# Half of a layer's weights loaded and narrowed later, more places for experts' weights, and an integer in the cosine's range reduction

## The chip, the core and the metric

One core of a Trainium2 chip. A kernel's time is the device time of one execution in microseconds, and what counts is the median of the runs. A profiled execution leaves a trace: its span runs from the first to the last instruction. Engines: PE multiplies matrices (PEld is its weight load), DVE and ACT work on vectors, SP issues the DMAs here.

## The reference

Three stages follow one another. q, k, v are 4 x 12 x 448 x 64, w1 8 x 768 x 1024, w2 8 x 1024 x 768, w_in 768 x 2048 and w_out 2048 x 768; w_in and w_out come as float64.

```python
scores = q @ k.T / sqrt(64) - log(448)
x = sigmoid(scores) @ v                     # 4 x 12 heads, then tokens: 1792 x 768
logits = x @ phi                            # 1792 x 32 slots, 8 experts of 4 slots
d = softmax(logits, axis=0); slots = d.T @ x
slot_out[e] = relu(slots[e] @ w1[e]) @ w2[e]   # 8 experts
x = softmax(logits, axis=1) @ slot_out      # combine weights c
h = x @ w_in
out = (h * cos(h)) @ w_out
```

The kernel never forms the second x: it multiplies slot_out (32 x 768) with w_in to m (32 x 2048), and gets h of 128 features and 448 tokens with one matmul of m and the turned combine weights.

## The kernel before

**Attention, about 0 to 157 us.** 24 pairs of heads, each with scores (L397), a sigmoid on ACT (L405) and the product with v (L416). A planner (`Plan`) gets operations with a cost and their predecessors, simulates the engines and emits each engine's instructions in the order of its simulation; `RANK` says which kind goes first. Into this order `fill(t)`, called twice for each pair, puts half loads of weights (`load_half`, 512 KB) and narrowing steps of w_in. A float64 is narrowed to float32 by one ACT instruction (L266) and three of DVE (L269, L270, L273) on pieces of 512 columns: 24 pieces for the whole of w_in. The places for loads are a pool of `W_SLOTS` tiles of 1 MB, through which raw w_in and then w1 pass; a place is free again when its w_in is narrowed. Narrowed w_in stays in `wi`, 48 KB of each partition.

**Experts, about 157 to 243 us.** The list `wloads` gives the order of all loads, `spots` the place of each. Seven more loads follow when attention leaves its memory (three places a, one more w, ct, m4 and zone); from there on each load waits for a place that PE has read. `w1_group` (L974) and `w2_rows` (L1010) run over two groups of four experts. `turn_weights` (L299, L305, L308) turns the combine weights of a batch; it stands inside group 1's loop over w1.

**Last layer, from about 245 us.** `wide_m` (L938) multiplies the features 0 to 511 of m, `rest_m` (L947) the other 1536, in four column blocks of 384; the latter are split into a high and a low part and spread over m4's partitions by 16 DMAs (`spread`, L1152). A unit is 128 features of one batch of 448 tokens. Its wave: `hidden` (L1208, PE), `scaled` (L1181, ACT: turns plus a quarter), `rounded` (L1184, ACT: adds 1.5 x 2^23), `centred` (L1188, DVE), `sined` (L1193, ACT), `times` (L1198 or L1200, DVE); from unit 4 on g is split into two fp16 halves, `upper` (L1217, ACT) and `lower` (L1221, DVE). Then `out_tile` (L1243) adds six tiles of w_out times g in six PSUM banks, one fp32 product for the units 0 to 3 and three fp16 products afterwards. A second planner orders all this; waves are put in three units ahead of their tiles, and hidden values take turns in two PSUM banks.

Rows of w_out are loaded into six places, narrowed (`wo_abs`, `wo_steps`) and split into fp16 (`wo_hi` L1122, `wo_lo` L1125), each once, ahead of the first unit that uses it. The order of units decides when: features 0 to 3 of batch 0, 0 to 5 of batch 1, all 16 of batch 2, the rest of batch 0, the rest of batch 1, all of batch 3. Where the batch changes, six banks are evicted (L1266 adds an earlier sum, L1270 to L1274 don't), and finished ones go out. `bound` to `keep_powers` work out a power of two that g is scaled with.

Of the kernel before, what the change touches and what calls it, by code (L numbers as in the profile page):

```python
# [12 lines left out]
U32 = mybir.dt.uint32  # L13
AF = mybir.ActivationFunctionType
# [20 lines left out]
W_SLOTS, A_SLOTS = 15, 3  # L35
# [7 lines left out]
W_SCALE, G_BITS = 8.0, 14  # L43
F64_SCALE = 2.0 ** -112
# [18 lines left out]
class Op:  # L63
# [11 lines left out]
class Plan:  # L75
# [3 lines left out]
    RINGS = {"sc": 3}  # L79
# [81 lines left out]
def fused(ctx: ExitStack, tc: tile.TileContext, qk, vv, phi, w1, w2, w_in, w_out, out):  # L161
# [8 lines left out]
    bias_s = const.tile([P, 1], F32, name="bias_s")  # L170
    run_z = const.tile([P, 1], F32, name="run_z")
# [12 lines left out]
    wloads = [("wi", 0, c, k) for c in range(KD) for k in range(2)]  # L184
# [5 lines left out]
    spots = ["w"] * (2 * KD + W_SLOTS - LATE) + slots_a[0:1] + ["w"] * LATE + slots_a[1:] + ["ct", "m4", "zone"]  # L190
# [3 lines left out]
    wloads.insert(2 * KD + W_SLOTS + A_SLOTS + 2, wloads.pop(2 * KD + 2 * KD - 1))  # L194
# [116 lines left out]
    with ExitStack() as at:  # L311
# [371 lines left out]
        pieces = [(c, n) for c in range(KD) for n in range(DFF // CV)]  # L683
# [9 lines left out]
        def attention():  # L693
# [184 lines left out]
        with tc.manual_schedule():  # L878
# [8 lines left out]
            nc.gpsimd.memset(bias_s, neg_log_s)  # L887
            warm = const.tile([P, 1], F32, name="warm")
# [64 lines left out]
    def slots_of(c):  # L953

        if c < 4:
            return l_all[:, 256 + c * NS:256 + (c + 1) * NS]
        return s_acc[:, 512 + (c - 4) * NS:512 + (c - 3) * NS]

    with ExitStack() as ex:
# [3 lines left out]
        with tc.manual_schedule():  # L963
# [133 lines left out]
    more_wo.append(ctx.enter_context(reuse("more_wo", bufs=1, side="right")))  # L1097
    stg = ctx.enter_context(reuse("stg", bufs=3))
# [46 lines left out]
    mh, ml = [ring[:, (12 + k) * S:(12 + k) * S + 3 * P] for k in range(2)]  # L1145

    def spread(js, groups):

        for j in js:
            cols = slice(MC + 3 * P * j, MC + 3 * P * (j + 1))  # L1150
            for g in groups:
                nc.sync.dma_start(  # L1152
                    out=m4[g * NS:(g + 1) * NS, cols].bitcast(F32), in_=(mh, ml)[g // 2][j * NS:(j + 1) * NS]
                )

    def m_split_hi():
        nc.scalar.copy(mh.bitcast(F32R), m_ps[2][:, 0:3 * P])
        spread([0], (0, 1))

    def m_split_lo():  # L1160
        nc.vector.tensor_sub(ml.bitcast(F32R), m_ps[2][:, 0:3 * P], mh)
        spread([0], (2, 3))
        spread(range(1, 4), range(4))

    SOME, PLAIN = (4, 6), 4
    units = [(t, f) for t in range(2) for f in range(SOME[t])] + [(2, f) for f in range(NF)]
    units += [(t, f) for t in range(2) for f in range(SOME[t], NF)]
    units += [(t, f) for t in range(3, B) for f in range(NF)]
# [4 lines left out]
    def buf(k):  # L1173
        return ring[:, k * S:(k + 1) * S]
# [329 lines left out]
```

## Time and profile before

| | us |
|---|---|
| median of 3 runs (493.5 to 493.74) | 493.56 |
| the profiled execution | 494.58 |
| its span | 492.7 |
| PE busy | 467.9 |
| DVE busy | 330.4 |
| ACT busy | 291.4 |

[...] The share of busy time is a mean over three stages with different limits, and a matmul's end is modelled: what a change is worth is read in its stage.

### The profile page before, as it was taken

The page shows a single profiled execution, that of the slowest core. Times are in us where ns is not written, and L with a number is a line of the kernel's source. Part 1 is how long each engine was busy: PE and PEld are TensorE (multiplying, and loading weights), DVE is VectorE, ACT ScalarE, POOL GpSimd, SP SyncE. Part 2 cuts the span into 40 slices and gives each one's busy share as a digit, 9 for nine tenths or more (in the row PEclk, how much of TensorE's full clock was granted, in tenths as well). Part 3 has the DMA queues.
Part 4 walks back from the last instruction along what each step waited for, and adds up shares of the span by engine and source line. Part 5 has one row for each costly group of instructions (what it writes and reads, how often), then busy time and mean ns, then how long its engine had stood idle before and what let it go on. Part 6 is the DMA issues. An engine that isn't in the chain of part 4 may idle for free.

```text
span 492.7 us, 11063 instructions
## 1 busy us (share of the span) xinstructions
PE 467.9 (95%) x4564; PEld 248.7 (50%) x4564; DVE 330.4 (67%) x665; ACT 291.4 (59%) x508; POOL 0.7 (0%) x7
## 2 busy tenths in 40 slices
PE   7999989999999998687899999999999999999996
PEld 5665556566566332223455555555555555555553
DVE  4898879999986155000189999999845575575553
ACT  5887848968864012000269889886756556655562
POOL 0000000000000000000000000000000000000000
PEclk9999999999999998989999999999999999999999
DMA  8989979989848999999944631300300030030003
GB/s 279 365 305 338 310 258 323 351 250 363 274 175 296 395 414 414 414 416 405 396 159 122 243 120 73 129 1 2 112 1 0 1 112 2 1 113 0 1 0 113
DMA packets 33442, 99.12 MB, mean 201 GB/s; under 512 B 3568, under 2 KB 17520, under 8 KB 33392
## 3 DMA queue, kind: packets, MB, share of 16 engines
q1 hardware_dynamic: 33392, 98.42, 54.7%
q8 instruction: 36, 0.59, 0.5%
q14 instruction: 14, 0.11, 0.1%
HBM read 92.11 MB, written 5.51 MB: 198 GB/s over the span
## 4 chain that ended last, share of the span: by engine, by line
PE 71%; DMA 17%; DVE 8%; ACT 2%; issue 1%; SPq 0%; ACTq 0%
PE o L1243 45%; DMA w<-in_w 13%; PE av L416 9%; PE sc L397 5%; PE h L1208 3%; DMA v<-in_vv 2%; PE h L974 2%; PE sl L635 2%; DMA raw<-in_qk 2%; DVE lo L378 1%; ACT a L405 1%; PE o L1228 1%; DVE xt L426 1%; PE m L947 1%; DVE hi L375 1%
## 5 line engine op out<-in xcount | busy, mean ns | idle before, releaser
L1243 PE MATMUL o<-gh,wh 128*128 128x448 f16 x360 | 127.4, 354 | 0.0
L1243 PE MATMUL o<-gl,wh 128*128 128x448 f16 x360 | 126.9, 352 | 0.0
L1243 PE MATMUL o<-gh,wl 128*128 128x448 f16 x360 | 126.9, 352 | 0.0
L1243 PEld LDWEIGHTS <-wh 128*128 128x128 f16 x720 | 70.3, 98 | 71.8 <-issue 11.1
L405 ACT ACTIVATE a<-sc,bias_s 128x896 f32<-128x896 f32 x72 | 71.2, 1008 | 26.7 <-PE sc L397 19.4
L416 PE MATMUL av<-a,v 128*64 128x224 f32 x576 | 60.4, 357 | 2.6 <-DMA v<-in_vv 1.7
L1221 DVE TENSOR_TENSOR gl<-wi,gh 128x448 f16<-128x448 f32 x60 | 37.4, 623 | 32.7 <-ACT gh L1217 32.2
L1217 ACT CAST gh<-wi 128x448 f16<-128x448 f32 x60 | 33.7, 562 | 41.9 <-PE o L1243 31.1
L416 PEld LDWEIGHTS av<-a,v 128*64 128x64 f32 x576 | 39.3, 137 | 22.9 <-issue 4.1
L1200 DVE SCALAR_TENSOR_TENSOR wi<-h,scales,wi 128x448 f32<-128x448 f32 x60 | 40.9, 681 | 13.6 <-ACT wi L1193 12.3
L1243 PEld LDWEIGHTS <-wl 128*128 128x128 f16 x360 | 35.3, 98 | 28.1 <-issue 0.6
L1193 ACT ACTIVATE wi<-wi 128x448 f32<-128x448 f32 x63 | 36.2, 575 | 21.8 <-DVE wi L1188 21.6
L1188 DVE SCALAR_TENSOR_TENSOR wi<-wi 128x448 f32<-128x448 f32 x63 | 39.2, 622 | 12.9 <-ACT wi L1184 12.9
L1010 PE MATMUL so<-w,zone 128*32 128x256 f32 (+1 forms) x256 | 36.2, 534 | 9.6 <-DMA w<-in_w 9.5
L1184 ACT ACTIVATE wi<-wi 128x448 f32<-128x448 f32 x63 | 36.3, 577 | 1.7
L1181 ACT ACTIVATE wi<-h 128x448 f32<-128x448 f32 x63 | 33.7, 535 | 5.0 <-PE h L1208 4.9
L397 PE MATMUL sc<-hi 64*64 64x448 f16 (+1 forms) x384 | 33.6, 337 | 2.9 <-ACT a L405 2.1
L397 PEld LDWEIGHTS <-hi 64*64 64x64 f16 x768 | 24.9, 106 | 21.9 <-issue 13.3
L1208 PE MATMUL h<-ct,m 128*128 128x448 f32 x64 | 33.6, 525 | 0.3 <-DVE m L1143 0.3
L397 PE MATMUL sc<-lo,hi 64*64 64x448 f16 (+1 forms) x384 | 33.0, 326 | 0.1
L397 PE MATMUL sc<-hi,lo 64*64 64x448 f16 (+1 forms) x384 | 32.9, 326 | 0.0
L1041 DVE COPY l_all<-ps_so 128x64 f32<-128x64 f32 x2 | 0.4, 224 | 47.9 <-PE ps_so L1034 47.9
(174 smaller groups left out, 543.8 us busy)
## 6 DMA issues: line engine op xcount, KB each, us to landing
w<-in_w SPq DMA_DIRECT2D x28, 768.0 KB, 15.4
w<-in_w SPq DMA_DIRECT2D x30, 512.0 KB, 5.7
wi<-in_w_in SPq DMA_DIRECT2D x24, 512.0 KB, 7.3
wo<-in_w_out SPq DMA_DIRECT2D x16, 768.0 KB, 5.9
w<-in_w SPq DMA_DIRECT2D x11, 1024.0 KB, 9.3
raw<-in_qk SPq DMA_DIRECT2D x48, 224.0 KB, 5.2
v<-in_vv SPq DMA_DIRECT2D x24, 224.0 KB, 4.8
out_t<-wi SPq DMA_DIRECT2D x24, 224.0 KB, 2.0
```

The lines of the kernel that those rows point to most:

```text
L397: nc.tensor.matmul(ps[to, j, 0:cols.stop - cols.start], keys[at, first:first + D], q[at, cols], **flags)
L405: nc.scalar.activation(a, ps, AF.Sigmoid, bias=bias_s, scale=qk_scale)
L416: nc.tensor.matmul(av[i][rows[j], k, 0:S // 2], v32[i][at, vc:vc + D], a[at, j, sides[k] if g < 3 else slice(0, S // 2)], start=g == 0, st ...
L1010: nc.tensor.matmul(e2[g, k][j * NS:(j + 1) * NS, 0:n], h1[g][:, c, j * NS:(j + 1) * NS], w(j), start=c == 0, stop=c == F // P - 1,)
L1181: nc.scalar.activation(tmp[u][0][:, cols], hs[u][:, cols], AF.Copy, bias=0.25, scale=inv2pi)
L1184: nc.scalar.activation(tmp[u][1][:, cols], tmp[u][0][:, cols], AF.Copy, bias=magic)
L1188: nc.vector.scalar_tensor_tensor(out=ph[:, cols], in0=tn[:, cols], scalar=-magic, in1=ph[:, cols], op0=ALU.add, op1=ALU.subtract)
L1193: nc.scalar.activation(tmp[u][1][:, cols], tmp[u][0][:, cols], AF.Sin, scale=-2.0 * math.pi)
L1200: nc.vector.scalar_tensor_tensor(out=g[:, cols], in0=hs[u][:, cols], scalar=g_scale, in1=tn[:, cols], op0=ALU.mult, op1=ALU.mult)
L1208: nc.tensor.matmul(h, m4[:, f * P:(f + 1) * P], ct4[:, t * S:(t + 1) * S], start=True, stop=True)
L1221: nc.vector.tensor_sub(gs[u][2], gs[u][0], gs[u][1])
L1243: nc.tensor.matmul(ps, w[:, cols], g, start=begins(u) and n == 0, stop=ends(u) and n == len(terms) - 1)
```

## The change

- w_in's first half (features 0 to 1023, `EARLY` = 8 blocks) goes through attention as before; `wi` shrinks to 24 KB of each partition, and `W_SLOTS` grows from 15 to 18. Six loads less stand ahead of w1 in `wloads`. `fill` narrows 12 pieces instead of 24 at half the pace, and its half loads have the pace 1 instead of 9/8 for each t.
- w_in's second half is loaded in the last layer, six chunks of 1 MB through two places: two right at its start, the others when a place has been narrowed. Twelve pieces are narrowed there, after the units 20 and 25 of the emission order. `late_products` multiplies them, three chunks at a time, `late_add` sums, `late_hi` and `late_lo` split and spread over m4.
- `rest_m` has four blocks of 128 columns.
- Units: features 0 to 3 of batch 0, 0 to 7 of batch 1, 4 to 7 of batch 0, 0 to 7 of the batches 2 and 3, then 8 to 15 of the batches 3, 2, 1, 0. That makes nine stretches instead of six; each batch's last stretch adds to the earlier sum on DVE, and all other evictions are ACT's.
- The scale is worked out twice, for each half of the features.
- The cosine: `turns` writes h / 2 pi + 1/4 as int32 (ACT), `centred` takes h / 2 pi minus that integer (DVE, from PSUM), the sine adds pi / 2 from a pointer operand. `rounded` goes, and a wave has two buffers instead of three.
- `turn_weights` moves from group 1 of w1 to the first two calls of `w2_rows`.

```diff
-W_SLOTS, A_SLOTS = 15, 3
+W_SLOTS, A_SLOTS = 18, 3
+EARLY = NF // 2
+LATE_W, LATE_C = (NF - EARLY) * P // 4, 3
+SCALE_AT, LATE_AT = 1, {20: range(3), 25: range(3, 6)}
...
-    wi = wip.tile([P, KD, DFF], F32, name="wi")
+    wi = wip.tile([P, KD, EARLY * P], F32, name="wi")
...
-    wloads = [("wi", 0, c, k) for c in range(KD) for k in range(2)]
+    wloads = [("wi", 0, c, 0) for c in range(KD)]
...
-                while len(done) < min(len(pieces), 23 * t // 44):
+                while len(done) < min(len(pieces), 23 * t // 88):
                     narrows(len(done))
-                while len(half) < min(2 * len(pieces) + 4, 4 + 9 * t // 8):
+                while len(half) < 4 + t:
                     h = len(half)
                     k = h // 2 - W_SLOTS
-                    if h >= 2 * (W_SLOTS - LATE + 2 * KD) or 2 * k + 1 >= len(done):
+                    if h >= 2 * (W_SLOTS - LATE + KD) or 2 * k + 1 >= len(done):
                         return
...
         for j in range(4):
-            at = MC + 3 * P * j
+            at = MC + P * j
             nc.tensor.matmul(
-                m_ps[2][j * NS:(j + 1) * NS, 0:3 * P], so, wi[:, c, at:at + 3 * P],
+                m_ps[2][j * NS:(j + 1) * NS, 0:P], so, wi[:, c, at:at + P],
...
+    def late_products(c):
+        ps = late_ps[c] = ps_h.tile([P, 512], F32, tag="h", name=f"late_m{c}")[:, 0:LATE_W]
+        for k in range(c + 1 - LATE_C, c + 1):
+            for j in range(4):
+                nc.tensor.matmul(
+                    ps[j * NS:(j + 1) * NS], both[k], late_w[k][:, j * LATE_W:(j + 1) * LATE_W],
+                    start=k == c + 1 - LATE_C, stop=k == c,
+                )
...
-    def scaled(u, cols):
-        nc.scalar.activation(tmp[u][0][:, cols], hs[u][:, cols], AF.Copy, bias=0.25, scale=inv2pi)
-    def rounded(u, cols):
-        nc.scalar.activation(tmp[u][1][:, cols], tmp[u][0][:, cols], AF.Copy, bias=magic)
+    def turns(u, cols):
+        nc.scalar.activation(tmp[u][1][:, cols].bitcast(I32), hs[u][:, cols], AF.Copy, bias=0.25, scale=inv2pi)
 
     def centred(u, cols):
...
         nc.vector.scalar_tensor_tensor(
-            out=ph[:, cols], in0=tn[:, cols], scalar=-magic, in1=ph[:, cols], op0=ALU.add, op1=ALU.subtract
+            out=ph[:, cols], in0=hs[u][:, cols], scalar=inv2pi, in1=tn[:, cols].bitcast(I32),
+            op0=ALU.mult, op1=ALU.subtract,
         )
 
     def sined(u, cols):
-        nc.scalar.activation(tmp[u][1][:, cols], tmp[u][0][:, cols], AF.Sin, scale=-2.0 * math.pi)
+        nc.scalar.activation(tmp[u][1][:, cols], tmp[u][0][:, cols], AF.Sin, bias=quarter, scale=2.0 * math.pi)
...
+        def late(c):
+            x = Op("sp", 2.5, lambda: late_load(c), [wide.get((c - 2, 1))]) if c > 1 else None
+            for n in range(2):
+                x = Op("act", .58, lambda n=n: late_narrow(c, n), [x, wide.get(c // LATE_C - 1)])
+                for cost in (.35, .605, .605):
+                    x = Op("dve", cost, lambda: late_steps[c].pop(0)(), [x])
+                wide[c, n] = x
...
             tiles(u, range(2))
+            if u == SCALE_AT:
+                scaling(0)
+            for c in LATE_AT.get(u, ()):
+                late(c)
             if u + 3 < n_units:
                 wave_ops(u + 3)
...
         for f in range(A_SLOTS, WO_SLOTS):
             load_wo(f)
+        for c in range(2):
+            late_load(c)
```

## Rows read from the trace of the kernel before

**Rows 1.** Page, the 40 slices: busy tenths of PE, and GB/s.

```profile
PE   7999989999999998687899999999999999999996
...
GB/s 279 365 305 338 310 258 323 351 250 363 274 175 296 395 414 414 414 416 405 396 159 122 243 120 73 129 1 2 112 1 0 1 112 2 1 113 0 1 0 113
```

**Rows 2.** Page, chain that ended last, by engine.

```profile
PE 71%; DMA 17%; DVE 8%; ACT 2%; issue 1%; SPq 0%; ACTq 0%
```

**Rows 3.** Windows: from:to us, length, busy (xcount) by engine, PEclk, DMA share, GB/s.

```profile
20.00:140.00 120.00, 114.84 (x2125) 71.61 (x2123) 109.32 (x283) 93.50 (x152) 0.00 (x0) 1.00 0.89 307
152.00:190.00 38.00, 37.06 (x396) 15.23 (x392) 17.89 (x39) 4.85 (x11) 0.00 (x0) 1.00 1.02 406
190.00:239.00 49.00, 37.95 (x263) 12.99 (x262) 3.14 (x7) 1.61 (x4) 0.00 (x0) 0.93 1.02 408
246.00:347.80 101.80, 101.80 (x541) 53.86 (x542) 96.67 (x158) 85.47 (x154) 0.00 (x0) 1.00 0.30 104
347.80:400.00 52.20, 52.20 (x274) 26.83 (x272) 32.13 (x53) 31.37 (x61) 0.00 (x0) 1.00 0.15 54
```

**Rows 4.** Page, DMA issues of weights.

```profile
w<-in_w SPq DMA_DIRECT2D x30, 512.0 KB, 5.7
wi<-in_w_in SPq DMA_DIRECT2D x24, 512.0 KB, 7.3
```

**Rows 5.** Groups by shape, DVE, 0 to 163 us: busy us, mean ns, idle before.

```profile
L270 DVE SCALAR_TENSOR_TENSOR wi<-wi,wi 128x512 uint32<-128x512 uint32 x24 | 16.4, 682 | 0.3
L273 DVE SCALAR_TENSOR_TENSOR wi<-wi,wi 128x512 uint32<-128x512 uint32 x24 | 16.3, 680 | 0.2
...
L269 DVE TENSOR_SCALAR wi<-wi 128x512 uint32<-128x512 uint32 x24 | 10.0, 418 | 3.0 <-ACT wi L266 3.0
```

**Rows 6.** Timeline of PE, two waits: start us, us, what, [idle before].

```profile
20.73 2.49 PE L416 MATMUL av<-a,v 128*64 128x224 f32 x24 [0.63 <-DMA v<-in_vv]
...
44.01 2.49 PE L416 MATMUL av<-a,v 128*64 128x224 f32 x24 [1.04 <-DMA v<-in_vv]
```

**Rows 7.** Timeline, start of the last layer.

```profile
252.34 1.47 PE L947 MATMUL m<-wi,s_acc 128*32 128x384 f32 x16
...
254.86 0.62 DVE L1198 TENSOR_TENSOR wi<-h,wi 128x448 f32<-128x448 f32 x1
...
256.32 0.92 PE L1243 MATMUL o<-wi,wo 128*128 128x448 f32 x2
...
257.17 0.38 PE L1294 MATMUL scale<-ident,scales 128*1 128x128 f32 x2
```

**Rows 8.** Timelines of PE and DVE, units 4 to 25 of the last layer.

```profile
271.77 0.35 PE L1243 MATMUL o<-gh,wh 128*128 128x448 f16 x1
...
299.27 0.95 DVE L1125 SCALAR_TENSOR_TENSOR wl<-wo,wh 128x768 f16<-128x768 f32 x1
...
345.94 0.62 DVE L1221 TENSOR_TENSOR gl<-wi,gh 128x448 f16<-128x448 f32 x1
346.48 0.95 DVE L1125 SCALAR_TENSOR_TENSOR wl<-wo,wh 128x768 f16<-128x768 f32 x1
...
347.80 0.35 PE L1243 MATMUL o<-gh,wh 128*128 128x448 f16 x1
```

**Rows 9.** Chain in order of time, 392 to 404 us.

```profile
396.43 3.42 PE o L1243 x18
...
400.20 3.42 PE o L1243 x18
```

**Rows 10.** Groups by shape, DVE, 244 to 492.7 us.

```profile
L1200 DVE SCALAR_TENSOR_TENSOR wi<-h,scales,wi 128x448 f32<-128x448 f32 x60 | 40.9, 681 | 13.6 <-ACT wi L1193 12.3
L1188 DVE SCALAR_TENSOR_TENSOR wi<-wi 128x448 f32<-128x448 f32 x63 | 39.2, 622 | 12.9 <-ACT wi L1184 12.9
...
L1198 DVE TENSOR_TENSOR wi<-h,wi 128x448 f32<-128x448 f32 x3 | 1.9, 619 | 0.6 <-ACT wi L1193 0.6
```

**Rows 11.** The same for ACT.

```profile
L1184 ACT ACTIVATE wi<-wi 128x448 f32<-128x448 f32 x63 | 36.3, 577 | 1.7
```

More of the change, by code (lines that the diff above doesn't have):

```diff
@@ L1024, in w2_rows @@
                     load_w()
+                for b in (c, c + 1) if g == 0 and c < B else ():
+                    turn_weights(ps_h, "h", b)
             def w2_out(g, k):
@@ L1160, in m_split_lo @@
     def m_split_lo():
[L1161 to L1168, printed above, removed]
+        nc.vector.tensor_sub(ml.bitcast(F32R), m_ps[2][:, 0:P], mh)
+        spread(mh, ml, MC, P, [0], (2, 3))
@@ new lines, in m_split_lo, with late_load, late_narrow @@
+        spread(mh, ml, MC, P, range(1, 4), range(4))
+    late_raw, late_w, late_steps, late_ps = {}, {}, {}, {}
+    def late_load(c):
+        late_raw[c] = latep.tile([P, DFF - EARLY * P, 2], U32, tag="raw", name=f"late{c}", bufs=2)
+        nc.sync.dma_start(
+            out=late_raw[c].rearrange("p m t -> p (m t)"), in_=w_in[c * P:(c + 1) * P, EARLY * P:].bitcast(U32)
+        )
+    def late_narrow(c, n):
+        if n == 0:
+            late_w[c] = latep.tile([P, DFF - EARLY * P], F32, tag="w", name=f"late_w{c}", bufs=LATE_C)
+        cols = slice(n * CV, (n + 1) * CV)
+        late_steps[c] = narrow(late_w[c][:, cols], late_raw[c][:, cols], late_w[c][:, cols])
@@ L1169, in fused @@
+    borders = [0]
+    for t, low, high in stretches:
+        borders.append(borders[-1] + high - low)
     gs, acc, sums = {}, {}, {}
@@ L1285, in bound, with scale_of @@
+    scales = gp.tile([P, 2, 4], F32, tag="scales", name="scales", bufs=1)
+    row = gp.tile([1, P + 4], F32, tag="row", name="row", bufs=1)
+    tops = {}
+    def scale_of(u):
+        k = units[u][1] // EARLY
+        return scales[:, k, 0:1], scales[:, k, 1:2]
+    def bound(k):
+        most = scales[:, k, 2:3]
+        if k:
+            nc.vector.tensor_reduce(out=most, in_=m_rest[:, 2], axis=AX.X, op=ALU.max, apply_absolute_value=True)
+            return
         nc.vector.tensor_reduce(
-            out=scales[:, 2:3], in_=m4[:, 0:MC].bitcast(F32), axis=AX.X, op=ALU.max, apply_absolute_value=True
+            out=most, in_=m4[:, 0:MC].bitcast(F32), axis=AX.X, op=ALU.max, apply_absolute_value=True
@@ L1287, in bound @@
         )
-        nc.vector.tensor_reduce(out=scales[:, 3:4], in_=mh, axis=AX.X, op=ALU.max, apply_absolute_value=True)
-        nc.vector.tensor_max(scales[:, 2:3], scales[:, 2:3], scales[:, 3:4])
+        nc.vector.tensor_reduce(out=scales[:, k, 3:4], in_=mh, axis=AX.X, op=ALU.max, apply_absolute_value=True)
+        nc.vector.tensor_max(most, most, scales[:, k, 3:4])
         nc.vector.memset(row[:, 0:P], 1.0)
-    def bound_row():
-        steps["scale"] = ps_h.tile([P, 512], F32, tag="h", name="scale")
-        nc.tensor.matmul(steps["scale"][0:1, 0:P], scales[:, 2:3], ident, start=True, stop=True)
@@ L1296, in powers, with bound_row @@
-    def powers():
-        top, (s, back) = row[:, P:P + 1], (row[:, P + k:P + k + 1] for k in (2, 3))
-        nc.vector.tensor_reduce(out=top, in_=steps["scale"][0:1, 0:P], axis=AX.X, op=ALU.max)
+    def bound_row(k):
+        tops[k] = ps_h.tile([P, 512], F32, tag="h", name="tops")
+        nc.tensor.matmul(tops[k][0:1, 0:P], scales[:, k, 2:3], ident, start=True, stop=True)
+    def powers(k):
+        top, (s, back) = row[:, P:P + 1], (row[:, P + j:P + j + 1] for j in (2, 3))
+        nc.vector.tensor_reduce(out=top, in_=tops.pop(k)[0:1, 0:P], axis=AX.X, op=ALU.max)
@@ L1305, in powers, with powers_all, keep_powers @@
         nc.vector.tensor_scalar_mul(back, top, 2.0 ** -G_BITS / W_SCALE)
-    def powers_all():
-        nc.tensor.matmul(
-            steps["scale"][:, P:P + 2], row[:, 0:P], row[:, P + 2:P + 4], start=True, stop=True
-        )
-    def keep_powers():
-        nc.vector.tensor_copy(scales[:, 0:2], steps.pop("scale")[:, P:P + 2])
+    def powers_all(k):
+        tops[k] = ps_h.tile([P, 512], F32, tag="h", name="powers")
+        nc.tensor.matmul(tops[k][:, 0:2], row[:, 0:P], row[:, P + 2:P + 4], start=True, stop=True)
+    def keep_powers(k):
+        nc.vector.tensor_copy(scales[:, k, 0:2], tops.pop(k)[:, 0:2])
     plan = Plan()
@@ L1423, in fused @@
             wide_m(both[c], c, [1])
-        rounded(0, first)
         centred(0, first)
-        scaled(0, second)
+        turns(0, second)
         sined(0, first)
-        rounded(0, second)
         wo_steps(0)
```

142 lines of the change are left out of this document (82 added, 60 removed).

## The prediction

> **What bounds the kernel now.** I read the page's first two parts, then the busy time by stage, the chain of waits by engine, the DMA issues, and at last single timelines. The reader should first see in the slices [rows 1] three stages: about 160 us of attention, a stretch where the GB/s row stands at 395 to 416, and from the 21st of the 40 slices on a last layer in which PE stays at 9 tenths until the last slice. The chain gives PE 71%, DMA 17% and DVE 8% [rows 2]. By stage [rows 3]:
>
> - 20 to 140 us, attention: PE busy 114.84 of 120 us, DVE 109.32. PE sets the pace; DVE is nearly full as well.
> - 152 to 239 us, experts: the DMA engines are full (share 1.02, 406 and 408 GB/s), DVE does almost nothing, PE is busy 37.95 of the last 49 us and waits for weights. This stretch is as long as its bytes.
> - 246 to 347.8 us, first part of the last layer: PE 101.80 of 101.80, DVE 96.67, ACT 85.47. PE bounds it, DVE is 5% behind. From 347.8 on PE is still full, but DVE drops to 32.13 of 52.20.
>
> The profiled run took 494.58 us, 492.7 in its span and 1.9 around it; the median of three is 493.56, so I take 1.0 off the sum at the end.
>
> **Fewer bytes in the full stretch.** Before, 24 half loads of w_in of 512 KB each and 28 halves of w1 pass during attention (30 loads of 512 KB have the name w, two of them the last of w2) [rows 4]. After, the limit in `fill` is 46 halves: 12 of w_in and 34 of w1. So 17 tiles of w1 instead of 14 lie ready when attention ends, and 3 x 1.0486 = 3.146 MB no longer pass in the full stretch: 3.146 MB / 407 GB/s = **7.7 us**. It can't be less unless the engines cease to be full; the seven loads that follow attention's end are the same seven, and w2's loads wait for w1 places that PE leaves faster than DMA fills. What is late next there? PE, but it has 49 - 37.95 = 11 us without work in the second half of this stretch, and warming matmuls besides, so after 7.7 us less DMA still ends last. The moved transposes of the combine weights go from group 1 to a place where PE waits anyhow: nothing.
>
> [...]
>
> **Attention.** Half of the narrowing goes: 12 pieces of 0.418 + 0.682 + 0.680 = 1.78 us of DVE [rows 5], 21 us of its 109, and an ACT instruction each. Loads fall from 52 to 46 halves, and each step issues 1 instead of 1.125. PE's idle time in 20 to 140 us is 5.16 us: that is the most there is to gain; two waits for v (0.63 and 1.04 us [rows 6]) are DMA's, the rest lies mostly in short waits behind DVE and ACT. The least is nothing, as the waits can come from order instead of load. I take a third, **1.7 us**. The time passes on, since the seven loads start when attention leaves their places.
>
> **Start of the last layer.** `rest_m` multiplies 128 instead of 384 columns. Two of its six chunks take 1.47 us [rows 7], all six 4.4, so 2.9 us leave this place. PE doesn't keep all of it: unit 1 needs product(1), which starts on DVE at 254.86, 1.46 us ahead of unit 1's first matmul at 256.32 [rows 7]. In front of it DVE is busy with w_out's narrowing, which stays; only the split of the rest gets shorter (384 to 128 columns, some 0.3 us). Product(1), which ended at 255.48, would end between 255.2 and, if the split no longer waits for PE's sums, 254.7; unit 1 then starts 1.1 to 1.6 us sooner. The sums come sooner by most of the 2.9, so I take **1.5 us**.
>
> **Added to PE in the last layer.** Nothing covers these, PE is full:
> - `late_products`: two groups, 6 chunks x 256 columns, the same 2.9 us that left above: **+2.9**.
> - `scaling(1)`: two small steps; the first of those of before takes 0.38 us [rows 7]: up to 0.8, and with overlap **+0.6**.
> - Three more borders between stretches (8 instead of 5). Unit to unit takes (347.80 - 271.77) / 21 = 3.62 us [rows 8]; across the border at 396.43 to 400.20 it takes 3.77 [rows 9]: 0.15 each, **+0.5**. The 18 additional evictions run on DVE and ACT in time that PE doesn't wait for.
>
> **DVE's budget in the last layer.** The one place where this can go wrong. Per unit, `centred` (0.622), `times` (0.681) and `lower` (0.62) [rows 8, 10] remain. `rounded`, 0.577 of ACT [rows 11], goes, which DVE doesn't feel directly; the sine's bias becomes a pointer (some 0.06 to 0.1 of ACT, judged by `times` with and without one, 0.681 and 0.619 [rows 10]); ACT is left freer than before. `centred` reads h from PSUM and an integer: the plain product that also reads h takes 0.619 against 0.622 for `centred` of before [rows 10], so I count 0. No row has the integer; its bounds are 0 and the 0.06 of the pointer form.
>
> *Units 8 to 11.* f = 6 and 7 were needed at units 16 and 17, now at 10 and 11. The eighth weight split ended at 299.27 + 0.95 = 300.2; unit 11 starts at 271.77 + 7 x 3.62 = 297.1 [rows 8], after the change 1.5 sooner: 4.6 us short. But the schedule prepares three units ahead, so that two to three waves of 1.7 us can be done later, and DVE has 5.1 us idle in 246 to 347.8, partly waits for the ACT work that goes. Stall 0 to 1.2 us; **+0.5**.
>
> *Units 25 to 39.* Before, w_out's last split ended at 347.43, just ahead of unit 25 at 347.80 [rows 8]. Now f = 15 is needed at unit 39, 14 x 3.62 = 50.7 us later, 53 with what PE gets added. In this time DVE has 14 waves more (27.0 us by their full durations), 12 late pieces (21.4), 6 evictions that add (4.1) and some 2.5 of sums, maxima and powers: 55. Full durations overstate it: in the full stretch `lower` at 345.94 is followed after 0.54 us by the next start though it is booked with 0.62 [rows 8]; 0.08 off some 90 instructions leaves 48. So 5 us to spare, or 2 us short at the other bound; I take 0 for the stall.
>
> *Late loads.* 6 x 1 MB in a stretch with 104 GB/s [rows 3]: hidden. Two wait in SP's queue behind w_out's loads and ahead of the 16 spreads of m, some 5 us; what waits for those spreads is the hidden matmul of unit 8, over 20 us on.
>
> **Sum.** -7.7 - 1.7 - 1.5 + 2.9 + 0.6 + 0.5 + 0.5 = **-6.4**: 494.6 - 6.4 = 488.2 by the profiled run, **487.2 us** by the median.
>
> **Rivals.** About 0.2% (1 us) can be told from no change here.
>
> 1. *As summed*, 485 to 489.5: chance 0.62.
> 2. *Attention gives more*: DVE and DMA were behind most of its 5.16 us, and no stall at unit 11: 482 to 485. For it: DVE at 91% of the stretch. Against: the two DMA waits come early, where the loads' pace hardly falls. 0.12.
> 3. *DVE becomes the bound of the last layer*, at unit 11 or 39, and PE waits 2 to 5 us: 489.5 to 492.5. For it: 0.4 us was all there was at unit 25. Against: the count above, and that the rows f = 8 to 13 of w_out can be worked on as soon as their six places are free, so DVE need not idle. 0.13. [...]
> 4. *The experts' stretch doesn't shrink*, because the additional places are not full when attention ends or something in front of unit 0 waits for w_out's loads instead: 493 to 494.5. Against: the full queue through all of it. 0.05.
> 5. *Slower*, and by one mechanism: `centred` with an integer operand costs far more than a float one. 40 of them lie ahead of unit 39. With 5 us to spare there and 6.4 to lose, it decides at 11.4 / 40 = 0.29 us more each, 0.91 instead of 0.62; at 1.0 (0.38 more) PE would wait 40 x 0.38 - 5 = 10 us and the time be 497.4. Nothing in the trace prices an integer beside a float; the narrowing's pure integer instructions cost what float ones do. 0.08.
>
> Range for 8 in 10: 483 to 491.5, which leaves out the far half of rival 2, the end of 3, and 4 and 5. Faster 0.87 (1, 2, 3), same 0.05 (4), slower 0.08 (5).
>
> **What would show it.** The stretch at over 400 GB/s should be nearly 8 us shorter at the same rate; else step one is wrong. PE's idle time in attention should be 3 to 4 us instead of 5. Between first and last fp16 unit PE should have no idle time but the two late groups of about 1.4 us, with DVE over 90% until unit 39 and at some 60% after. If PE waits for DVE around units 8 to 11 or 32 to 39, rival 3 holds; the mean of the new `centred` decides rival 5.

## The result and the profile after

The changed kernel took 500.09 us against 493.65 of the kernel before beside it, ratio 1.0124 (95% interval 1.0091 to 1.0156): slower by 1.2%, where 487.2 and the range 483 to 491.5 were forecast. One of its six executions was disturbed; the ratio and all that is worked out from it leave that one out, and the median of the other five is 499.05. The profiled execution took 501.99 us, 500.2 in its span. Busy time by stretch, with the columns of [rows 3]:

```profile
20.00:140.00 120.00, 113.48 (x2127) 70.87 (x2120) 96.38 (x254) 88.03 (x142) 0.00 (x0) 1.00 0.86 291
190.00:232.70 42.70, 33.36 (x278) 11.38 (x270) 7.81 (x14) 0.86 (x2) 0.00 (x0) 1.00 1.02 410
240.00:342.00 102.00, 98.42 (x543) 52.16 (x533) 94.09 (x167) 71.20 (x126) 0.00 (x0) 1.00 0.43 152
342.00:400.00 58.00, 54.94 (x298) 27.34 (x296) 49.24 (x82) 36.11 (x65) 0.00 (x0) 1.00 0.09 23
```

The full stretch (190.00 to 232.70) is shorter at the same rate as in [rows 3], as forecast. In the last layer DVE is busy 94.09 of 102.00 us, about as much as in [rows 3], but PE, which had no gap there, now lacks 3.6 us from 240 to 342 and 3.1 from 342 to 400.

In the changed kernel the last layer's lines are `hidden` L1258, `turns` L1233, `centred` L1237, the sine L1243, `times` L1250, `upper` L1267 (it writes gh), `lower` L1271 (it writes gl), `out_tile` L1293, the evictions that add L1310, the late narrowing L277, L278 and L281 on late_w, the late products L1195.

Two rows of PE bound the stages, the last products that wait for a weight and the first fp16 product (unit 4):

```profile
232.73 1.07 PE L1016 MATMUL so<-w,zone 128*32 128x512 f32 x8 [2.12 <-DMA w<-in_w]
...
264.29 0.35 PE L1293 MATMUL o<-gh,wh 128*128 128x448 f16 x1
```

Before, they start at 239.02 and at 271.77 [rows 8]. So unit 4 comes 7.48 us sooner, but unit 63, by the same kind of row, starts at 492.67 instead of 485.38. Stage by stage against the forecast:

```
us                                   before   after    change  forecast
start to end of attention            163.00   164.58    +1.58    -1.7
to last products that wait for DMA    76.02    68.15    -7.87    -7.7
to unit 4                             32.75    31.56    -1.19    -1.5
unit 4 to unit 63                    213.61   228.38   +14.77    +4.5
unit 63 to the end of the span         7.32     7.53    +0.21     0
```

The groups of DVE and of ACT by shape from 275 to 480 us answer to [rows 10] and [rows 11]:

```profile
L1237 DVE SCALAR_TENSOR_TENSOR wi<-h,wi 128x448 f32<-128x448 f32 x53 | 32.4, 617 | 1.3 <-ACT wi L1233 1.2
...
L1243 ACT ACTIVATE wi<-wi,quarter 128x448 f32<-128x448 f32 x52 | 34.2, 664 | 21.1 <-DVE wi L1237 20.9
L1267 ACT CAST gh<-wi 128x448 f16<-128x448 f32 x53 | 30.0, 567 | 63.2 <-PE o L1293 55.2 <-DVE wi L1250 5.6 <-DVE wi L1310 2.5
L1233 ACT ACTIVATE wi<-h 128x448 int32<-128x448 f32 x53 | 28.5, 540 | 3.1 <-PE h L1258 3.0
```

`centred` with its integer, and now with h from PSUM, takes 617 ns (622 before): the two together cost nothing, and rival 5 falls. The sine with a pointer takes 664 (575 before). But ACT's `gh` row has 63.2 us of idle time in front of it, 55.2 of them behind PE. The same row of the kernel before, which I had not read:

```profile
L1217 ACT CAST gh<-wi 128x448 f16<-128x448 f32 x57 | 32.0, 562 | 41.1 <-PE o L1243 31.1 <-DVE wi L1200 9.1 <-DVE wo L273 0.8
```

**Where the last layer loses.** The steady period of a unit is 3.62 us [rows 8]. Taking the starts of the units' first fp16 products one by one, the changed kernel exceeds it by 1.2 us at units 10 and 11, by 9.9 in units 20 to 27 (late products 2 x 1.50 and the two steps of the second scaling 2 x 0.38 are PE's own work; 6.1 is waiting), and by 0.97 to 1.01 at each border at units 32, 40, 48 and 56. Before, the two borders where all six evictions add cost 0.22 and 0.21, and no other unit is over.

A loss in units 20 to 27 in the timeline of ACT, then DVE, then PE:

```profile
324.68 0.67 ACT L1243 ACTIVATE wi<-wi,quarter 128x448 f32<-128x448 f32 x1
329.30 0.56 ACT L1267 CAST gh<-wi 128x448 f16<-128x448 f32 x1 [3.94 <-PE o L1293]
...
330.35 0.52 ACT L1233 ACTIVATE wi<-h 128x448 int32<-128x448 f32 x1
...
325.96 0.68 DVE L1250 SCALAR_TENSOR_TENSOR wi<-h,scales,wi 128x448 f32<-128x448 f32 x1
...
327.42 0.42 DVE L1204 COPY m_rest<-late_m 128x256 f32<-128x256 f32 x1
329.89 0.63 DVE L1271 TENSOR_TENSOR gl<-wi,gh 128x448 f16<-128x448 f32 x1 [2.05 <-ACT gh L1267]
...
334.93 0.68 DVE L1250 SCALAR_TENSOR_TENSOR wi<-h,scales,wi 128x448 f32<-128x448 f32 x1
...
324.66 1.50 PE L1195 MATMUL late_m<-late_w,s_acc 128*32 128x256 f32 x24
326.69 0.47 PE L1258 MATMUL h<-ct,m 128*128 128x448 f32 x1 [0.53 <-DVE wi L1250]
...
335.66 0.47 PE L1258 MATMUL h<-ct,m 128*128 128x448 f32 x1 [1.45 <-DVE wi L1250]
...
348.56 1.50 PE L1195 MATMUL late_m<-late_w,s_acc 128*32 128x256 f32 x24 [0.65 <-DVE wi L1250]
...
355.81 0.47 PE L1258 MATMUL h<-ct,m 128*128 128x448 f32 x1 [1.02 <-DVE wi L1250]
...
359.73 0.47 PE L1258 MATMUL h<-ct,m 128*128 128x448 f32 x1 [0.59 <-DVE scales L1361]
```

From 325.36 to 329.30 ACT does nothing: it stands in front of the `upper` of unit 22 (3.94 us). gh and gl have two places each, so this `upper` needs the place of unit 20, which PE has not released; unit 20 took long because PE had given 1.50 us to the late products at 324.66 and had waited 0.53 us for an earlier `times` at 326.69. DVE, whose next instruction is the `lower` behind that `upper`, stands for 2.05 us. The `turns` of unit 23 could have run once its hidden product was done (326.69 + 0.47 = 327.16), but stands behind the `upper` in ACT's queue and starts at 330.35. Its `times` comes at 334.93, and PE waits 1.45 us for it ahead of the hidden product at 335.66. Not all of this delay is ACT's: between 330.48 and 334.93 DVE puts 3.9 us of the late narrowing ahead of this wave's `centred` and `times`. PE waits for a `times` again at 348.56 (ahead of the second late products) and 355.81, and for the second scaling at 359.73.

The border at unit 40, where the stretch of the units 32 to 39 ends and its six banks are evicted, ACT and then DVE and PE:

```profile
399.52 0.56 ACT L1267 CAST gh<-wi 128x448 f16<-128x448 f32 x1 [2.49 <-PE o L1293]
400.00 0.54 ACT L1233 ACTIVATE wi<-h 128x448 int32<-128x448 f32 x1
401.32 0.67 ACT L1243 ACTIVATE wi<-wi,quarter 128x448 f32<-128x448 f32 x1 [0.78 <-DVE wi L1237]
403.15 0.56 ACT L1267 CAST gh<-wi 128x448 f16<-128x448 f32 x1 [1.16 <-PE o L1293]
403.62 0.54 ACT L1233 ACTIVATE wi<-h 128x448 int32<-128x448 f32 x1
404.94 0.67 ACT L1243 ACTIVATE wi<-wi,quarter 128x448 f32<-128x448 f32 x1 [0.78 <-DVE wi L1237]
...
405.64 0.68 DVE L1250 SCALAR_TENSOR_TENSOR wi<-h,scales,wi 128x448 f32<-128x448 f32 x1 [0.74 <-ACT wi L1243]
406.25 1.27 DVE L1310 SCALAR_TENSOR_TENSOR extra<-o,scales,extra 128x448 f32<-128x448 f32 x2
407.43 0.61 DVE L1271 TENSOR_TENSOR gl<-wi,gh 128x448 f16<-128x448 f32 x1
407.96 2.46 DVE L1310 SCALAR_TENSOR_TENSOR extra<-o,scales,extra 128x448 f32<-128x448 f32 x4
...
408.69 0.35 PE L1293 MATMUL o<-gh,wh 128*128 128x448 f16 x1 [0.20 <-DVE extra L1310]
```

Each `turns` stands directly behind a `gh` that waited for PE. So a wave's `times` comes at 405.64, after 0.74 us of waiting for the sine; the first eviction stands behind it and starts at 406.25, 3.1 us after unit 39 began on PE (403.14), and a `gl` lies between the second and the third. PE waits for `extra`.

### The profile page after: what moved, and what is told of

It is laid out like the page before. It is cut to its first block, busy times and chain, and to the rows that moved or that the text cites. A ratio compares the mean times of both kernels' runs of the same rounds, so it can differ in the third digit from the quotient of the medians.

```text
span 500.2 us, 11145 instructions
## 1 busy us (share of the span) xinstructions
PE 467.7 (93%) x4616; PEld 249.4 (50%) x4616; DVE 338.0 (68%) x687; ACT 265.3 (53%) x450; POOL 0.8 (0%) x8
## 4 chain that ended last, share of the span: by engine, by line
PE 67%; DVE 12%; DMA 11%; ACT 6%; issue 2%; SPq 0%; DVEq 0%; ACTq 0%
PE o L1293 32%; PE av L424 11%; PE sc L405 7%; DMA w<-in_w 7%; PE h L982 4%; DMA v<-in_vv 4%; PE h L1258 3%; ACT a L413 2%; DVE extra L1310 2%; PE sl L643 2%; DVE gl L1271 2%; PE so L1016 1%; DVE wi L1237 1%; DVE wi L1250 1%; PE o L1278 1%
## 5 line engine op out<-in xcount | busy, mean ns | idle before, releaser
L1293 PE MATMUL o<-gh,wh 128*128 128x448 f16 x360 | 127.4, 354 | 1.0 <-DVE extra L1310 0.6
L1293 PE MATMUL o<-gl,wh 128*128 128x448 f16 x360 | 126.8, 352 | 0.5 <-DVE gl L1271 0.5
L1293 PE MATMUL o<-gh,wl 128*128 128x448 f16 x360 | 126.9, 352 | 0.0
L1293 PEld LDWEIGHTS <-wh 128*128 128x128 f16 x720 | 70.3, 98 | 73.2 <-issue 10.8
L1267 ACT CAST gh<-wi 128x448 f16<-128x448 f32 x60 | 34.0, 567 | 68.0 <-PE o L1293 59.9
L1271 DVE TENSOR_TENSOR gl<-wi,gh 128x448 f16<-128x448 f32 x60 | 37.3, 622 | 33.7 <-ACT gh L1267 33.2
L1243 ACT ACTIVATE wi<-wi,quarter 128x448 f32<-128x448 f32 x63 | 41.6, 665 | 26.2 <-DVE wi L1237 25.9
L1250 DVE SCALAR_TENSOR_TENSOR wi<-h,scales,wi 128x448 f32<-128x448 f32 x60 | 40.5, 680 | 14.4 <-ACT wi L1243 14.1
L1293 PEld LDWEIGHTS <-wl 128*128 128x128 f16 x360 | 35.3, 98 | 29.6 <-issue 2.0
L1237 DVE SCALAR_TENSOR_TENSOR wi<-h,wi 128x448 f32<-128x448 f32 x63 | 38.5, 616 | 1.8 <-ACT wi L1233 1.6
L1016 PE MATMUL so<-w,zone 128*32 128x512 f32 (+1 forms) x256 | 31.1, 490 | 8.9 <-DMA w<-in_w 8.8
L1258 PE MATMUL h<-ct,m 128*128 128x448 f32 x64 | 33.3, 520 | 4.8 <-DVE wi L1250 3.6
L1233 ACT ACTIVATE wi<-h 128x448 int32<-128x448 f32 x63 | 33.9, 540 | 4.5 <-PE h L1258 4.4
L386 DVE TENSOR_TENSOR lo<-raw,hi 128x448 f16<-128x448 f32 x48 | 28.5, 614 | 0.3
L434 DVE COPY xt<-av 128x448 f32<-128x448 f32 x24 | 14.9, 622 | 18.5 <-PE av L424 18.2
```

The costliest lines, as they stand in the source:

```text
L1016: nc.tensor.matmul(e2[g, k][j * NS:(j + 1) * NS, 0:n], h1[g][:, c, j * NS:(j + 1) * NS], w(j), start=c == 0, stop=c == F // P - 1,)
L1233: nc.scalar.activation(tmp[u][1][:, cols].bitcast(I32), hs[u][:, cols], AF.Copy, bias=0.25, scale=inv2pi)
L1237: nc.vector.scalar_tensor_tensor(out=ph[:, cols], in0=hs[u][:, cols], scalar=inv2pi, in1=tn[:, cols].bitcast(I32), op0=ALU.mult, op1=ALU.s ...
L1243: nc.scalar.activation(tmp[u][1][:, cols], tmp[u][0][:, cols], AF.Sin, bias=quarter, scale=2.0 * math.pi)
L1250: nc.vector.scalar_tensor_tensor(out=ph[:, cols], in0=hs[u][:, cols], scalar=scale_of(u)[0], in1=tn[:, cols], op0=ALU.mult, op1=ALU.mult)
L1258: nc.tensor.matmul(h, m4[:, f * P:(f + 1) * P], ct4[:, t * S:(t + 1) * S], start=True, stop=True)
```

## The experiments

All are edits of the changed kernel unless it is said that they start from the kernel before; each was timed beside the kernel before, and "by the ratios" compares two kernels by their ratios to it. After every edit the planner makes its order anew. "4 to 63" is the time from unit 4 to unit 63, "20 to 27" what these units (and 19, where the late products fall there) take over 3.62 us each (3.8 of it PE's own added work), "border" what one of the borders at 40, 48 and 56 (before: 39 and 49) takes over it.

```
kernel            us      ratio (95%)               4 to 63  20 to 27  border
before            493.65                            213.61     0.0     0.2
changed           500.09  1.0124 (1.0091 to 1.0156)  228.38     9.9     1.0
no_narrow         500.38  1.0132 (1.0083 to 1.0182)  229.34    11.2     1.0
spread_late       497.27  1.0078 (1.0050 to 1.0106)  227.19     9.7     1.0
three_places      487.32  0.9874 (0.9822 to 0.9926)  217.91     4.6     0.0
three_again       487.71  0.9865 (0.9835 to 0.9895)  217.84     4.6     0.0
before_three      493.20  1.0002 (0.9981 to 1.0022)  213.16     0.0     0.0
cos_alone         495.44  1.0032 (1.0005 to 1.0059)  215.96     0.6     1.0
cos_three         493.13  0.9983 (0.9963 to 1.0003)  213.28     0.0     0.0
float_cos         490.46  0.9966 (0.9939 to 0.9994)  220.69     6.4     0.3
float_cos_three   488.64  0.9885 (0.9850 to 0.9919)  219.24     5.9     0.0
plan_pe           504.12  1.0229 (1.0180 to 1.0278)  232.23    12.7     1.6
turns_first       497.84  1.0070 (1.0040 to 1.0101)  228.01    11.2     0.0
borders_first     495.73  1.0024 (0.9998 to 1.0050)  225.61    10.0     0.0
no_products       493.07  0.9969 (0.9931 to 1.0008)  220.77     3.2     1.0
no_scale2         495.75  1.0048 (1.0023 to 1.0073)  225.37     7.3     1.0
three_spread      490.17  0.9922 (0.9896 to 0.9947)  218.82     5.6     0.0
slots15           495.94  1.0055 (1.0030 to 1.0081)  218.54     5.3     0.0
```

**Is it DVE's additional work?** no_narrow leaves the 36 steps of the late narrowing out; spread_late releases the blocks one by one.

```diff
-                for cost in (.35, .605, .605):
-                    x = Op("dve", cost, lambda: late_steps[c].pop(0)(), [x])
```
```diff
-SCALE_AT, LATE_AT = 1, {20: range(3), 25: range(3, 6)}
+SCALE_AT, LATE_AT = 1, {15: [0], 17: [1], 19: [2], 21: [3], 23: [4], 25: [5]}
```

> The changed kernel without the 36 VectorE steps that narrow the second half of w_in (21.4 us of DVE); ScalarE's copy, the loads, the late products and all else stay, so that the second half of the features is not what the reference has. Theories A (order) and B (too much DVE work) both say that units 20 to 27 keep only PE's own added work of 3 to 3.6 us: 6 us less, 493 to 495 us. Theory C, the serial chain of late loads and the second scaling sets these units: at least 3 us of excess beyond 3.6 stay in units 25 to 27: 496 to 498. The borders of stretches at units 32, 40, 48 and 56 should still cost 1.0 us each, as their evictions don't depend on the narrowing.

> The changed kernel with the late row blocks of w_in released one by one at units 15, 17, 19, 21, 23 and 25 instead of three at 20 and three at 25. Theory A (order: six blocks of narrowing in VectorE's queue ahead of the wave): the loss in units 20 to 27 falls by 2 to 4 us, 496 to 498.5. Theory B (too much work until unit 32): the loss comes earlier or spread out, the sum stays within 1.5 us: 499 to 501. If PE waits for the late products instead (loads too late), it is over 501.

With 21.4 us less of DVE work the kernel is no faster, and units 20 to 27 lose more (11.2). Its `gh` row:

```profile
L1267 ACT CAST gh<-wi 128x448 f16<-128x448 f32 x53 | 30.0, 566 | 60.7 <-PE o L1293 55.5 <-DVE wi L1250 5.0
```

ACT's wait for PE is as long as ever, 55.5 us. In units 20 to 27 themselves DVE has only 2.7 us less to do (32.8 and then 30.1 us), because the plan puts the narrowing of w_out there instead; but from unit 25 to 39, the stretch of my budget, it falls from 47.7 to 31.5 us, and DVE is busy for 75% of units 20 to 27 while they lose more. So the theory that DVE has too much work is refuted, and with it rival 3 as I had put it. All three theories had forecast under 498: the order theory too was wrong in its form of then, in which the narrowing in DVE's queue holds up the wave. spread_late came out 0.45% under the changed kernel by the ratios, 2.3 us, inside the range of the order theory, but its last layer has only 1.2 of that and units 20 to 27 lose 9.7: bunching is at most a small part.

**A third place** for gh and gl. `upper` of unit u then waits for the products of unit u-3. before_three is the same edit in the kernel before.

```diff
-    gp = ctx.enter_context(reuse("gp", bufs=2))
+    gp = ctx.enter_context(reuse("gp", bufs=3))
...
-                g = Op("act", .5, lambda: upper(u), [mul[u], tile.get((u - 2, NO - 1))])
+                g = Op("act", .5, lambda: upper(u), [mul[u], tile.get((u - 3, NO - 1))])
```

> The changed kernel with three places instead of two for the fp16 halves gh and gl, so that ScalarE's `upper` of unit u waits for the products of unit u-3 and not u-2. In the changed kernel PE lost 6.3 us in units 20 to 27 beyond its own added work (units 20, 22, 25, 26 and 27 took 2.2, 1.7, 3.4, 1.6 and 0.9 us over the period of 3.62). Theory A, order: ScalarE stands behind an `upper` that waits for PE (3.9, 3.5 and 2.9 us), VectorE then waits for ScalarE (2.05 and 1.83 us) and PE in turn for VectorE. Then the third place takes 4 to 6 us of the 6.3 away: 494 to 496.5 us, and no ACT wait for PE over 2 us between 325 and 362. Theory B, VectorE simply has too much work in units 20 to 27: the loss moves but stays within 1.5 us: 498.5 to 501.

> The changed kernel with the third place once more, in more rounds and beside the same with the cosine of before: 486 to 488 us, 1.1 to 1.5% under the kernel before, 12 to 14 us under the changed kernel.

> The kernel before with three places for gh and gl and nothing else. If the third place merely mends what the change brought, the kernel before has only its four border losses of 0.07 and 0.15 us to win: 493.2 to 494.4 beside 494.2, no difference. Rival: the third place is a gain by itself and hides that the change is worth less than forecast: under 491.

By the ratios it gives 2.5 and 2.6% (12.3 and 12.8 us) against the changed kernel, more than the 4 to 6 that I expected, since it takes the borders and unit 10 too; what it gave in units 20 to 27 was 5.3. There DVE does the same work, 32.0 us beside 32.8, in 33.6 us instead of 38.9. The kernel before gains nothing. ACT's wait for PE in front of `gh` goes from 55.2 to 3.3 us:

```profile
L1267 ACT CAST gh<-wi 128x448 f16<-128x448 f32 x54 | 30.6, 566 | 25.3 <-DVE wi L1250 21.8 <-PE o L1293 3.3
```

At its border at unit 40, ACT and then DVE, the first eviction waits for PE and not for DVE's queue, and starts 0.8 us after unit 39 (391.89); PE loses nothing:

```profile
391.04 0.67 ACT L1243 ACTIVATE wi<-wi,quarter 128x448 f32<-128x448 f32 x1 [0.69 <-DVE wi L1237]
392.51 0.56 ACT L1267 CAST gh<-wi 128x448 f16<-128x448 f32 x1 [0.81 <-PE o L1293]
393.43 0.54 ACT L1233 ACTIVATE wi<-h 128x448 int32<-128x448 f32 x1 [0.35 <-PE h L1258]
...
391.74 0.68 DVE L1250 SCALAR_TENSOR_TENSOR wi<-h,scales,wi 128x448 f32<-128x448 f32 x1 [0.74 <-ACT wi L1243]
392.66 1.28 DVE L1310 SCALAR_TENSOR_TENSOR extra<-o,scales,extra 128x448 f32<-128x448 f32 x2 [0.23 <-PE o L1293]
```

**The integer cosine.** cos_alone and cos_three start from the kernel before; float_cos is the changed kernel with the old cosine and two places, float_cos_three with three. The core of the edit in cos_alone (float_cos is its reverse, with three buffers a wave and 23 x S of `extra`):

```diff
-        nc.scalar.activation(tmp[u][0][:, cols], hs[u][:, cols], AF.Copy, bias=0.25, scale=inv2pi)
...
+        nc.scalar.activation(tmp[u][1][:, cols].bitcast(I32), hs[u][:, cols], AF.Copy, bias=0.25, scale=inv2pi)
...
-            a = Op("act", .57, lambda: rounded(u, whole_s), [a])
```

> The kernel before with the cosine's whole turns as integers and nothing else of the change: `rounded` (0.577 us of ScalarE per unit) goes, `centred` reads h and an integer, the sine has a pointer for its bias. My theory: `centred` takes 0.61 to 0.63 us as before, PE was the bound and stays it, and the time is 492.5 to 493.7, at most 1 us less than before. Rival: the cosine is a part of the loss, by the sine's additional 0.09 us or by the order that the plan now makes: over 495.

> The changed kernel with the cosine of before (`scaled`, `rounded`, three buffers a wave, 23 instead of 19 additional buffers), and still two places for gh and gl. Theory: with `rounded` gone ScalarE arrives earlier at an `upper` that PE hasn't released, so the integer cosine made the four adding borders cost 1.0 us each (cosine alone in the kernel before: 1.01 at each of its two, 0.15 to 0.22 without). Then the borders at units 40, 48 and 56 cost 0.2 to 0.3 each again, 2 to 3 us less, and the time is 495 to 498; what units 20 to 27 lose stays within 2 us of 6.3. Rival: borders at 1.0 as before, because it is six evictions on VectorE in a row: 499 to 501, or more with ScalarE's 37 us of additional work.

> The kernel before with the integer cosine and a third place for gh and gl. The integer cosine with two places lost 0.3% there (1.01 us at each of two borders against 0.22, 0.5 at unit 24). With the third place that goes: 493 to 494 beside some 493.5, no difference, all units at 3.62. If the integer cosine has a price of its own (longer sine), it stays at 495.

> The changed kernel with the cosine of before and the third place. If the integer cosine does no harm once the third place is there, this is within 1 us of the kernel with the third place alone (487.3): 486.5 to 488.5. If ScalarE's 37 us of `rounded` less are worth something in units 20 to 27, it is 1 to 2 us slower, 488.5 to 490.

This is the surprise of the study. The cosine alone makes the kernel before slower by 0.32%: its two adding borders go from 0.2 to 1.0 us. With the old cosine put back the changed kernel is 1.6% faster by the ratios (7.8 us; 7.7 from unit 4 to 63): 490.46, below the 495 to 498 that I expected, and under the kernel before. The borders fall to 0.3 as expected; units 20 to 27, where I had expected at most 2 us, lose 3.5 us less. With three places the integer cosine does no harm (493.13) and its good can't be told by the times (487.71 against 488.64, intervals that overlap); the profiles have 1.4 us for it from unit 4 to 63, 1.3 of them in units 20 to 27. The rows of cos_alone and then of float_cos agree with the mechanism:

```profile
L1217 ACT CAST gh<-wi 128x448 f16<-128x448 f32 x56 | 31.6, 565 | 57.6 <-PE o L1243 53.9 <-DVE wi L1200 3.7
...
L1269 ACT CAST gh<-wi 128x448 f16<-128x448 f32 x54 | 30.5, 565 | 37.5 <-PE o L1295 23.2 <-DVE wi L1252 12.8 <-DVE wi L1240 0.9
```

With the integer cosine ACT has 0.58 us less to do in each unit (and 0.09 more in its sine) and spends the time in front of `upper` waiting for PE: 53.9 us against 31.1 in the kernel before, 55.2 against 23.2 in the changed one, with the next `turns` behind it.

**Is it the order?** plan_pe only changes the plan's price of a product; turns_first forces ACT's order; borders_first forces it from unit 29 on (its condition is `if u - 2 >= 29 and u - 2 in ups:`).

```diff
-                    "pe", .694 if u < PLAIN else .567, lambda o=o: out_tile(u, o), need
+                    "pe", .694 if u < PLAIN else .604, lambda o=o: out_tile(u, o), need
```
```diff
...
+            if u - 2 in ups:
+                a.next.append(ups[u - 2])
+                ups[u - 2].todo += 1
```

> The changed kernel with two places, where only the plan's price of a TensorE product changes, from 0.567 to the measured 0.604 us: another order, no other work. If the order is wrong because the plan takes PE for 6% faster than it is, ScalarE's waits for PE (55 us in 275 to 480) shrink and the time falls by 3 us or more, under 497. If two places are too few in any such order, it stays within 2 us of 500.

> The changed kernel with two places and another order alone: ScalarE does `turns` of unit u+2 before `upper` of unit u, so that the `upper` that waits for PE no longer holds up the start of a later wave. The same instructions and buffers. If the loss is the order on ScalarE, as I now believe (of the two forms of the cosine, the one with a ScalarE step less lost 9.6 us more), the adding borders cost under 0.4 us instead of 1.0, units 20 to 27 lose 3 us less, and the time is 488 to 493. If two places are too few whatever the order, it is over 496.

> The changed kernel with two places where ScalarE's order is forced (`turns` of unit u+2 ahead of `upper` of unit u) from unit 29 on alone. Forced everywhere, it took the borders at 32, 40, 48 and 56 from 4.0 to 0.2 us but cost 13 us in units 20 to 27. Forced here alone it should give the 3.5 to 4 us of the borders and change nothing before unit 28: 495.5 to 497. Rival: the borders lost nothing there because PE was late already, and they cost 1.0 again: 499.5 to 501.

A better price for PE made it worse, outside both forecasts: 504.12, the borders at 1.6 us. turns_first missed its time of 488 to 493 but told the two losses apart. Its groups on ACT:

```profile
L1269 ACT CAST gh<-wi 128x448 f16<-128x448 f32 x53 | 29.8, 561 | 0.8 <-DVE wi L1252 0.8
L1235 ACT ACTIVATE wi<-h 128x448 int32<-128x448 f32 x53 | 28.9, 545 | 64.6 <-PE h L1260 64.5
```

The wait of `gh` for PE is gone (0.8 us idle) and the borders cost nothing: there the order alone, with the same instructions and buffers, is the cause. But `turns` now waits for the hidden product, whose turn on PE comes late, and units 20 to 27 lose 11.2 and units 7 to 12 another 2.5 (1.2 in the changed kernel). Forced from unit 29 on alone, the order leaves units 20 to 27 at 10.0 and gives 2.8 us in the last layer (the borders' 3.8, of which 1.0 is lost again at units 60 to 62); the time is in the range that I expected.

**Units 20 to 27.** no_products leaves out PE's late products and fills the sums from the narrowed weights; no_scale2 uses the first power of two for both halves; three_spread is three_places with the late blocks of spread_late.

```diff
-            x = Op("pe", .44 * LATE_C, lambda: late_products(c), [wide[k, 1] for k in range(c + 1 - LATE_C, c + 1)], ring="h")
...
+            added = Op("dve", .35, lambda: (late_products(c), late_add(c)), [wide[k, 1] for k in range(c + 1 - LATE_C, c + 1)])
```
```diff
-                scaling(1, added)
+                scaled_by[1] = added
```

> The changed kernel with two places and without the two groups of late products on PE (the sums of the late features are filled from the narrowed weights instead, so the second half of the features is not the reference's). PE's own work falls by 3.0 us. If their place in PE's order and their bank of h's two set the loss in units 20 to 27, another 3 us or more go with them: 492 to 494.5. If not, only their own 3.0 go: 496.5 to 498.

> The changed kernel with two places and without the second scaling (the second half of the features uses the first half's power of two): PE's own work falls by some 0.6 us, VectorE's by 1.3. If its two steps in h's banks hold up the waves of units 25 to 27, which lost 5.9 us of which 1.5 are the late products, 3 us or more go there: 495 to 497.5. If not, under 1.5 us: 498.5 to 500.

> Three places, and the late row blocks released one by one at units 15 to 25. With three places 4.57 us of excess stay in units 20 to 26, of which 3.0 are the late products and about 0.8 the second scaling; at most 0.8 us is to be had: 486.5 to 488, no difference that can be told from three places alone.

Without the late products these units wait 2.4 us (3.2 less the scaling) instead of 6.1: 3.7 go beyond PE's own 3.0. Without the second scaling 4.3 remain (7.3 less 3.0). Both times lie in the ranges forecast for the case that such pauses set the loss. So PE's pauses start the greater part of the waiting; that ACT's queue is what multiplies them is read from the rows above, and no edit shows it in these units alone. three_spread, 490.17 where 486.5 to 488 was expected, is not better than three_places.

**The three places for experts' weights**, undone on top of three_places:

```diff
-W_SLOTS, A_SLOTS = 18, 3
+W_SLOTS, A_SLOTS = 15, 3
```

> The kernel with three places for gh and gl, and the 18 places for experts' weights put back to 15. My forecast priced the three places at 7.7 us by 3.146 MB at 407 GB/s: the experts' stretch from the end of attention to the last products that wait for a weight should grow from 68.0 to 75 to 76.5 us, the time from 487.3 to 494 to 495.5. Rival: places don't matter as much since half of w_in no longer passes through them: 488 to 491.

The last products that wait for a weight start at 237.26 and attention ended at 161.86, so the stretch took 75.4 us against 68.0 and 66.4 in the two profiles with 18 places. By the ratios the time is 1.8 to 1.9% over three_places, 9 us, a little above the 7.7, and the median lies 0.4 us above its range; 0.6 of the 9 us are in units 20 to 27 of the last layer.

```profile
237.26 1.06 PE L1016 MATMUL so<-w,zone 128*32 128x512 f32 x8 [1.02 <-DMA w<-in_w]
```

## Why the prediction was wrong, step by step

- *Experts* (-7.7): right. 7.87 us in the profiled run, 7.8 by the medians of the 13 profiles with the new attention and the four with the old one; slots15 takes them back.
- *Attention* (-1.7): not shown. The profiled run has +1.58, but it is the latest of the 13 profiles with this attention, whose end lies between 160.91 and 164.58, median 161.79; the four with the old one (three with another last layer) lie between 162.59 and 163.61, median 162.87. The medians differ by -1.1, less than the 13 scatter. PE's idle time from 20 to 140 us, for which I had named 3 to 4 us as the sign, is 6.52 in the profiled run (5.16 before) and 3.5 to 5.9 in the other twelve; DVE has 13 us less to do there, not 21.
- *Start of the last layer* (-1.5): 1.19; in all profiles of the changed start with the integer cosine 31.56 or 31.57 against 32.75. With the old cosine it is 31.25 or 31.26, the forecast 1.5, and the integer cosine alone makes the start of the kernel before 0.5 longer (33.23).
- *Late products* (+2.9) and *scaling* (+0.6): 3.00 and 0.76 us of PE.
- *Borders* (three more, +0.5): wrong. Four borders cost 1.0 each where two had cost 0.2. I priced a border from the kernel before [rows 9], by one of the two units that share its loss (0.15 of 0.22), and carried it into one with another order on ACT.
- *Stall at units 8 to 11* (+0.5, 0 to 1.2): 1.2, at the end of its bounds. Here ACT's `upper` does wait for DVE (1.02 us at 283.42 and 1.30 at 288.23), which is at w_out's narrowing, as forecast; with the third place the stall is 0, and 0.1 with the old cosine.
- *Stall at units 25 to 39* (0): this is the failed step. I made it a budget of DVE's busy time, and the budget was right: DVE was busy for 47.7 us from unit 25 to unit 39 (48 to 55 forecast), and its work isn't the limit, as no_narrow shows. Yet in these units PE lost 3.6 us beyond its own work at units 25 to 27 and 1.0 at the border at unit 32, and another 2.5 in units 20 to 24. What I held for slack (I had written of units 8 to 11 that "the schedule prepares three units ahead") was not there: with two places for gh and gl no wave is finished more than two units ahead, and the instruction that waits for the place stands in ACT's queue ahead of the `turns` of the next wave. I wrote that `rounded` "goes, which DVE doesn't feel directly" and that "ACT is left freer than before". With two places that freedom was the harm: the edit that I had costed at nothing is worth some 8 us of loss here (float_cos). Rival 5 named that edit, but by a price (at least 0.29 us more for each `centred`) that it doesn't have.

The rows at 324.68, 329.30 and 330.35 show ACT's queue: nothing passes the `upper` that waits 3.94 us, the `turns` of unit 23 neither, though its hidden product was done at 327.16. The gap that repeats is ACT's: `gh` waits for PE 37 times from 275 to 480 us, 55.2 us in all, and with a third buffer 3.3 us. My budget judged DVE by its occupancy; here DVE was busy for 84% of units 20 to 27 while PE lost 6.1 us to waiting, and for 95% with the third place while it lost 0.9.

With the third place the sum comes out: 217.9 us from unit 4 to 63, +4.3 against the forecast +4.5, and 487.3 and 487.7 us against the forecast 487.2. That it agrees so closely is partly luck: the borders and the stall at units 8 to 11 cost nothing instead of 0.5 each, the two borders of before give back 0.4, and 0.9 us of waiting in units 20 to 27 stand on the other side, with late products and scaling at 3.8 instead of 3.5. The forecast fits a kernel with one more place, and that kernel, 1.3% faster than the kernel before and 2.5% faster than the changed one, is the version to keep.

What stays open: why in units 20 to 27 the old cosine waits 2.7 us where the integer one waits 6.1, and why with three places it is the other way round (2.2 and 0.9). A third place also makes the plan anew, so that place and order aren't told apart there. That it's the order on ACT was shown at the borders alone; in these units another order (turns_first, plan_pe) made it worse, and none was found that mends them with two places.

## What to carry to other kernels

Before you call an engine's work hidden, look on every engine that feeds the bound one for its first instruction that waits for the bound engine itself, and count what stands behind it in the queue: the lead was the number of buffers here, not the number of units that the schedule prepares. Taking work off an engine that feeds made the kernel slower here (0.32% in cos_alone, 1.6% in the changed kernel against float_cos); at the borders (1.0 us each in the changed kernel, 0.0 in turns_first) because an order made by estimates let it arrive early at such a wait. One more buffer costs 1.8 KB a partition here and is the cheapest test for it.

## What the runs showed that I had not expected

- ACT with 36 us less to do (63 times 0.577 us [rows 11]; its sines take 5.6 us more) cost 0.3% in one kernel and 1.6% in the other with two places, and nothing with three.
- `centred` with an fp32 operand from PSUM and an integer one takes 617 ns, against 622 with two fp32 operands that ACT had written. The two were not tried apart.
- The end of attention varied by 3.7 us between profiles of the same instructions (160.91 to 164.58), so that a term of 1 us there can't be read from one profile.
